# Attention and expert layer on one core: the mixed query tile transposed with 128 rows, the last output tile projected with 128 columns

## The chip, the cores and the metric

The kernel runs on one core of a Trainium2 chip. The metric is the device time of one execution in microseconds (us). The time before is 489.7 us, the median of three runs (489.33 to 493.12).

## What is computed

Attention with pooled queries, followed by a mixture of experts. Batch 2, 8 heads, 1152 positions, head size 64; everything is float32.

```python
q_pool = q.reshape(B, H, S // 2, 2, D).mean(axis=3)            # 576 queries a head
scores = np.matmul(q_pool, k.transpose(0, 1, 3, 2)) / np.sqrt(D)
attn = softmax(scores)                                        # over 1152 keys
x = heads side by side of np.matmul(attn, v)                  # (1152, 512)
expert = argmax(x @ w_gate); gate = its softmax probability
out[i] = gate[i] * (relu(x[i] @ w1[expert]) @ w2[expert])     # 8 experts, 512 -> 1024 -> 512
```

An expert takes no more than 288 tokens, in the order of the tokens; a token past that gives zeros.

## The kernel before, in words

The attention stage works on eight pairs of heads (2 batches, 4 pairs each). A pair's 576 pooled queries are four tiles of 128 and a rest of 64 (`MIX`, line 45) for each head. The two rests of 64 share one tile, the mixed query tile: its first 64 rows belong to the first head of the pair, its last 64 to the second. So a pair has nine query tiles, and each is worked through in three rounds of 384 keys, 27 rounds a pair.

In a round (`rounds`, lines 686 to 749) TensorE issues, in an order written out by hand: some matmuls of transposed probabilities with values (`pv_kt`, line 434); the score matmuls of the round six ahead (`s_third`, line 371), two terms for a plain tile and three for the mixed one; and three transposes of probabilities (`t_round`, line 409). VectorE takes the maximum of each score third (line 376), ScalarE the exponential (line 392, three rounds ahead); a score buffer is free for a new third when its exponential is done, and there are four. ScalarE and VectorE take turns at copying transposed probabilities out (lines 420 and 418).

Between the rounds stands the preparation of the next pair: the keys are transposed in three parts (`prep_k`, line 217), the pooled queries in two (`prep_q`). The first part of `prep_q` transposes two full query tiles (line 243). The second (`r == 1`) transposes two more full ones (line 243) and then the rest (line 249): 64 rows, both heads' columns side by side, through the 64 x 64 corner of the identity. ScalarE copies 256 or 320 columns out (line 257), and VectorE and GpSimd split them into high and low parts (lines 267 and 273). The pooled queries themselves are sums of neighbours, made by GpSimd into the tile `qp` (lines 204 and 207; for the first pair by VectorE, lines 200 and 324). `qp` has one buffer, requested anew for each pair (line 195).

What leaves attention goes through `x_out` (lines 447 to 486): the products `xt`, copied from PSUM by ScalarE (line 442), are transposed back and multiplied with the gate's weights in one matmul a tile (line 464) against `wgi`, an identity of 128 columns with the 16 gate columns beside it. A float32 matmul is two matmul instructions in the trace. Each pair calls `x_out` twice: for query tiles 0 and 1 (two full tiles) at the end of its own rounds, and for tiles 2, 3 and the rest (two full tiles and one with 64 weight columns) in round 17 of the next pair. The last pair is taken apart (`TAIL`, line 640): its rest is a call of its own (group 3), at the end of attention. `xt` has 320 columns and two buffers. The copies behind `x_out` (lines 473 and 479, VectorE) read 128 rows of full tiles and 64 rows of the rest.

Routing (lines 488 to 560) follows per batch, on VectorE with two small matmuls (lines 523 and 524), and scatters the tokens to their experts' slots by GpSimd (line 551). Then come the experts (lines 839 to 978), whose weights stream in through SyncE's queue (line 620) into 16 buffers. How many blocks of tokens an expert has is known on the chip alone, so blocks behind the first stand under a branch (line 950).

The order of instructions is by hand on TensorE throughout; in the main rounds also on ScalarE and VectorE; in the expert stage on GpSimd, SyncE, ScalarE and TensorE. Elsewhere a planner orders them by estimated costs.

Of the kernel before, what the change touches and what calls it, by code (L numbers as in the profile page):

```python
# [8 lines left out]
F32 = mybir.dt.float32  # L9
# [22 lines left out]
def f32(ap):  # L32
    return ap.bitcast(F32)
# [3 lines left out]
def attention_moe(ctx: ExitStack, tc, cap, q, k, v, wg, w1, w2, out):  # L37
    nc = tc.nc
    B, H, S, D = q.shape
    SQ = S // 2  # L40
    E, DM, F = w1.shape
    P = 128
    KT = S // P
    QT = SQ // P
    MIX = SQ - QT * P
    NT = QT + 1
    G0 = 2 * P
    GW = (G0, SQ - G0)
    W = P + 2 * E
# [12 lines left out]
    ident = const.tile([P, P], F32, name="ident")  # L62
# [22 lines left out]
    wgi = const.tile([P, HP, W], F32, name="wgi")  # L85
# [31 lines left out]
    ld_p = a_ctx.enter_context(tc.tile_pool(name="ld", bufs=1))  # L117
# [3 lines left out]
    sm_p = a_ctx.enter_context(tc.tile_pool(name="sm", bufs=4))  # L121
# [66 lines left out]

    ready = {}
    qps = {}  # L190
    pool_ins = [None]

    def prep_pool(p):
        kraw, qraw, vraw = raws[p]
        qp = ld_p.tile([P, NT, 2, D], F32, tag="qp", name="qp")
        qo = qp.rearrange("p t h d -> p h t d")
        qps[p] = qp
        if p == 0:
            for t in (0, 2):
                nc.vector.tensor_tensor(  # L200
                    out=qo[:, :, t:t + 2], in0=qraw[:, :, t:t + 2, 0:D], in1=qraw[:, :, t:t + 2, D:2 * D], op=ALU.add
                )
            return
        nc.gpsimd.tensor_tensor(
            out=qo[0:MIX, :, QT], in0=qraw[0:MIX, :, QT, 0:D], in1=qraw[0:MIX, :, QT, D:2 * D], op=ALU.add
        )
        pool_ins[0] = nc.gpsimd.tensor_tensor(
            out=qo[:, :, 0:QT], in0=qraw[:, :, 0:QT, 0:D], in1=qraw[:, :, 0:QT, D:2 * D], op=ALU.add
        ).ins
# [27 lines left out]
    def prep_q(p, r):  # L237
        qp = qps[p]
        qa, qb = q1[p % nbuf]
        ps = m_ps.tile([P, 512], F32, tag="t", name="qps")  # L240
        sc = 1.0 / 16.0
        for i in range(2):
            nc.tensor.transpose(
                ps[:, i * P:(i + 1) * P], qp[:, 2 * r + i].rearrange("p h d -> p (h d)"), ident
            )
        n = 2 * P
        spans = [[(0, n, 2 * r * P)] for _ in range(2)]
        if r == 1:
            nc.tensor.transpose(
                ps[:, n:n + MIX], qp[0:MIX, QT].rearrange("p h d -> p (h d)"), ident[0:MIX, 0:MIX]  # L250
            )
            spans = ([(0, n + MIX, n)], [(0, n, n), (n, n + MIX, QT * P + MIX)])
            n += MIX
        qt_s = ld_p.tile([P, CW], F32, tag="qts", name="qts", bufs=2)

        def post():
            nc.scalar.activation(qt_s[:, 0:n], ps[:, 0:n], AF.Copy, scale=sc)

            def split(j, tl):
                ready[p] = ready.get(p, 0) + 1  # L260
                if True:
                    rs = slice(j * D, (j + 1) * D)
                    for r0 in (slice(0, D), slice(D, P)):
                        for a, z, o in spans[j]:
                            c = slice(o, o + z - a)
                            if p:
                                nc.vector.tensor_copy(tl[r0, 0, c], qt_s[rs, a:z])  # L267
                            else:
                                nc.scalar.copy(tl[r0, 0, c], qt_s[rs, a:z])
                    for r0 in (slice(0, D), slice(D, P)):  # L270
                        for a, z, o in spans[j]:
                            c = slice(o, o + z - a)
                            nc.gpsimd.tensor_tensor(  # L273
                                out=tl[r0, 1, c], in0=qt_s[rs, a:z], in1=f32(tl[rs, 0, c]), op=ALU.subtract
                            )

            return slot_of_dve(lambda: split(0, qa), lambda: split(1, qb))

        return post
# [147 lines left out]
    def pv_kt(p, grp, kt):  # L427
        vraw = raws[p][2]
        if kt == 0:
            pvps[0] = (t_ps if grp == 3 else v_ps).tile([P, 512], F32, tag="t" if grp == 3 else "v", name="pv")  # L430
        ps = pvps[0]
        src, c0, n, _ = GRP[grp]
        for j in range(2):
            nc.tensor.matmul(  # L434
                ps[j * D:(j + 1) * D, 0:n], vraw[:, j, kt, :], pts[p, j, src][:, kt, c0:c0 + n],
                start=kt == 0, stop=kt == KT - 1,
            )
        if kt == KT - 1:
            xt = sm_p.tile([P, GW[1]], F32, tag="xt", name="xt", bufs=2)

            def post():
                nc.scalar.copy(xt[:, 0:n], ps[:, 0:n])  # L442

            xts[p, grp] = xt
            return post

    def x_out(p, grp):
        b, hp = divmod(p, HP)
        sm = sums[p]
        cuts = GRP[grp][3]  # L450
        if cuts[-1] == LAST[0]:
            nc.gpsimd.tensor_copy(sm[0:MIX, QT, 1, 0:3], sm[MIX:P, QT, 0, 0:3])
        t0, t1 = cuts[0][0], cuts[-1][1]
        z = sm_p.tile([P, 3, 2], F32, tag="z", name="z")
        zr = z[:, 0:t1 - t0]
        nc.vector.tensor_reduce(out=zr, in_=sm[:, t0:t1, :, 0:3], axis=AX.X, op=ALU.add)
        nc.vector.tensor_scalar_add(zr, zr, 1e-9)
        nc.vector.reciprocal(zr, zr)
        xt = xts.pop((p, grp))
        ps = m_ps.tile([P, 512], F32, tag="t", name="xps")  # L460
        for t in range(t0, t1):
            i = t - t0
            w = P if t < QT else MIX
            nc.tensor.matmul(
                ps[0:w, i * W:(i + 1) * W], xt[:, i * P:i * P + w], wgi[:, hp, :], start=True, stop=True
            )

        def post():
            for a0, a1, rows in cuts:
                nt = a1 - a0  # L470
                src = ps[0:rows, (a0 - t0) * W:(a1 - t0) * W].rearrange("p (t w) -> p t w", w=W)
                zz = z[0:rows, a0 - t0:a1 - t0, :].unsqueeze(3)
                nc.vector.tensor_tensor(
                    out=lp[0:rows, b, a0:a1, :, 2 * hp:2 * hp + 2].rearrange("p t e h -> p t h e"),
                    in0=src[:, :, P:W].rearrange("p t (h e) -> p t h e", h=2),
                    in1=zz.to_broadcast([rows, nt, 2, E]),
                    op=ALU.mult,
                )
                nc.vector.tensor_tensor(
                    out=x_tok[0:rows, b, a0:a1, hp * P:(hp + 1) * P].rearrange("p t (h d) -> p t h d", h=2),  # L480
                    in0=src[:, :, 0:P].rearrange("p t (h d) -> p t h d", h=2),
                    in1=zz.to_broadcast([rows, nt, 2, D]),
                    op=ALU.mult,
                )

        return slot_of_dve(post)
# [91 lines left out]
    for done in range(0, E * cap, nz * P):  # L578
        n = min(nz * P, E * cap - done)
# [46 lines left out]
    with ExitStack():  # L626
        load_pair(0)
        prep_pool(0)
        first = prep_first()
        load_pair(1)  # L630
# [55 lines left out]
        def rounds(n0, n1):  # L686
            nonlocal posts
            for n in range(n0, n1):
# [32 lines left out]
                if 0 <= p < NP:  # L721
                    if i == XO0 and p < NP - 1:
                        todo.append(lambda: x_out(p, 0))
                    if i == 26 and p % HP == HP - 1 and p < NP - 1:
                        todo.append(lambda b=p // HP: routing(b, 0, 2))
                    if p + 1 < NP:
                        pk, pq, p0 = (PK, PQ, 1) if p else (PK0, PQ0, PP0)
                        if i in pk:
                            todo.append(lambda: prep_k(p + 1, pk.index(i)))
                        if i in pq:  # L730
                            todo.append(lambda: prep_q(p + 1, pq.index(i)))
                        if i == p0:
                            prep_pool(p + 1)
                        if i == 25:
                            todo.append(lambda: prep_mix(p + 1))
                    if p == 0 and i == 6:
                        todo.append(lambda: prep_mix(0))
                    if i == 10 and p + 2 < NP:
                        load_pair(p + 2)
                    if p in (1, 2) and i % 3 == 0:  # L740
                        fill()
                    while fills and p == 2 and i == NS - 1:
                        fill()
                    if p == NP - 2 and i % 2 == 0 and i // 2 < NR0:
                        load_w(i // 2)
# [258 lines left out]
```

## Time and profile before

| what | value |
|---|---|
| median of three runs | 489.7 us (489.33 to 493.12) |
| the profiled execution | 491.99 us |
| its span, first to last instruction | 490.3 us |
| mean granted TensorE clock | 0.974 of full speed |
| TensorE matmuls busy | 449.8 us, 92% |
| VectorE, ScalarE, GpSimd busy | 245.9, 251.1, 170.9 us |

The profile is of one execution. PE is TensorE's matmuls, PEld its weight loads, which overlap with matmuls; DVE is VectorE, ACT ScalarE, POOL GpSimd, SP SyncE. L464 is line 464 of the kernel. Matmuls are pipelined and their ends are modelled, so a busy TensorE isn't one at its peak.

### The profile page before, as it was taken

To read this page: it belongs to the slowest core of one execution; us is meant where nothing else is said; L and a number is where in the kernel's file an instruction comes from. 1 tells how busy PE (TensorE), PEld (TensorE's weight loads), DVE (VectorE), ACT (ScalarE), POOL (GpSimd) and SP (SyncE) were. 2 spreads that over 40 slices of the span, in tenths; PEclk is the share of its full clock that TensorE was granted. 3 is DMA by queue.
4 is the path that set the end of the run, shared out by engine and by line. 5 is a ranking of instruction groups with operands and counts; after the bars stand their busy time and mean duration, and the time that the engine had idled before them with its cause. 6 is when DMAs were issued, how large, how long until landed. Compare 5 with 4: busy or idle time off the path is not lost. (4 is left out here: it accounts for less than half of the span.)

```text
span 490.3 us, 9116 instructions
## 1 busy us (share of the span) xinstructions
PE 449.8 (92%) x3183; PEld 315.5 (64%) x3183; DVE 245.9 (50%) x725; ACT 251.1 (51%) x731; POOL 170.9 (35%) x290
## 2 busy tenths in 40 slices
PE   4779999999999999999999998996999999999990
PEld 3667777777677677677776765464668456674670
DVE  5687777777777999887777565010100011001100
ACT  5777887787787677777777761020221112101100
POOL 4477444344344454454433001522031133112110
PEclk9799999999999999999999999798999999999996
DMA  7998984033043044052104625699983093000000
GB/s 216 276 284 282 385 285 108 5 98 100 5 98 102 1 119 124 3 150 55 30 20 139 260 70 204 215 341 355 363 285 145 5 364 123 13 12 24 12 11 21
DMA packets 55737, 69.96 MB, mean 143 GB/s; under 512 B 21873, under 2 KB 32117, under 8 KB 55680
## 3 DMA queue, kind: packets, MB, share of 16 engines
q1 hardware_dynamic: 50320, 53.56, 35.5%
q0 software_dynamic: 4816, 15.66, 8.5%
q8 instruction: 32, 0.52, 0.4%
q14 instruction: 25, 0.20, 0.1%
q10 hardware_dynamic: 544, 0.02, 0.1%
HBM read 52.48 MB, written 11.98 MB: 131 GB/s over the span
## 5 line engine op out<-in xcount | busy, mean ns | idle before, releaser
L376 DVE TENSOR_REDUCE negm<-s 128x1 f32<-128x384 f32 x216 | 119.6, 554 | 56.9 <-PE s L371 55.8
L371 PE MATMUL s<-k,q 128*128 128x384 f32 x432 | 132.8, 390 | 9.6 <-ACT p L392 9.0
L392 ACT ACTIVATE p<-s,negm 128x384 f32<-128x384 f32 x216 | 125.0, 587 | 14.6 <-DVE negm L380 9.2
L409 PE MATMUL tp<-ident,p 128*128 128x128 f32 x648 | 106.8, 274 | 0.5 <-DVE pt L418 0.4
L371 PEld LDWEIGHTS s<-k,q 128*128 128x128 f32 x432 | 66.8, 194 | 45.3 <-ACT p L392 25.2
L409 PEld LDWEIGHTS tp<-ident,p 128*128 128x128 f32 x648 | 83.9, 141 | 10.0 <-issue 1.4
L420 ACT COPY pt<-tp 128x384 f32<-128x384 f32 (+1 forms) x160 | 69.3, 445 | 38.5 <-PE tp L409 35.5
L434 PE MATMUL pv<-pt,vraw 128*64 128x256 f32 (+2 forms) x612 | 85.4, 403 | 0.8 <-ACT xt L442 0.8
L273 POOL TENSOR_TENSOR q<-qts,q 64x256 fp32r<-64x256 f32 (+1 forms) x76 | 52.0, 693 | 55.0 <-DVE q L267 47.8
L229 POOL TENSOR_TENSOR k<-kts,k 64x384 fp32r<-64x384 f32 x42 | 44.8, 1068 | 53.7 <-DVE k L228 51.9
L890 PE MATMUL hps<-wraw,xf 128*64 128x256 f32 (+1 forms) x448 | 49.7, 390 | 8.1 <-PEq L950 4.6
L828 POOL DMA_INDIRECT out_dram<-yo,id x17 | 17.1, 1006 | 112.9 <-issue 42.5
L434 PEld LDWEIGHTS pv<-pt,vraw 128*64 128x64 f32 x612 | 36.3, 136 | 27.2 <-issue 10.6
L930 PE MATMUL yps<-wraw,ht 128*64 128x256 f32 (+1 forms) x448 | 48.1, 382 | 1.2 <-DVE ht L907 1.2
L895 DVE TENSOR_SCALAR hs<-hps 128x256 f32<-128x256 f32 x12 | 5.1, 425 | 87.9 <-PE hps L890 87.9
L890 PEld LDWEIGHTS hps<-wraw,xf 128*64 128x64 f32 (+1 forms) x448 | 30.5, 136 | 26.5 <-issue 7.5
L392 ACT ACTIVATION_READ_ACCUMULATOR p<-s,negm 128x1 f32 x216 | 44.5, 206 | 0.0
L418 DVE COPY pt<-tp 128x384 f32<-128x384 f32 (+1 forms) x80 | 40.0, 508 | 6.1 <-PE tp L409 6.0
L822 ACT ACTIVATE yo<-yps,gt 128x256 f32<-128x256 f32 (+1 forms) x15 | 7.7, 516 | 61.5 <-PE yps L930 31.1
L930 PEld LDWEIGHTS yps<-wraw,ht 128*64 128x64 f32 (+1 forms) x448 | 28.4, 133 | 16.8 <-ACT ht L909 1.8
L849 PEld LDWEIGHTS hps<-xf,wraw 128*128 128x128 f32 x192 | 21.7, 192 | 1.2 <-issue 1.2
L849 PE MATMUL hps<-xf,wraw 128*128 128x128 f32 x192 | 22.2, 277 | 0.0
(117 smaller groups left out, 377.0 us busy)
## 6 DMA issues: line engine op xcount, KB each, us to landing
wraw<-in_moe_w_dram SPq DMA_DIRECT2D x32, 1024.0 KB, 7.9
vraw<-in_v_dram SPq DMA_DIRECT2D x8, 576.0 KB, 4.0
kc<-k SPq DMA_DIRECT2D x16, 288.0 KB, 4.0
xs<-zrow POOLq DMA_DIRECT2D x4, 1032.0 KB
qraw<-in_q_dram SPq DMA_DIRECT2D x16, 256.0 KB, 3.6
kraw<-in_k_dram SPq DMA_DIRECT2D x14, 288.0 KB, 4.6
xe<-xs POOLq DMA_DIRECT2D x14, 258.0 KB, 6.0
out_dram<-zrow POOLq DMA_DIRECT2D x2, 1024.0 KB
```

What stands on the lines that cost most here:

```text
L229: nc.gpsimd.tensor_tensor(out=tl[rl, c], in0=kt_s[rh, :], in1=f32(tl[rh, c]), op=ALU.subtract)
L273: nc.gpsimd.tensor_tensor(out=tl[r0, 1, c], in0=qt_s[rs, a:z], in1=f32(tl[rs, 0, c]), op=ALU.subtract)
L371: nc.tensor.matmul(ps[:, 0:CW], a, w, start=i == 0, stop=i == len(terms) - 1)
L376: nc.vector.tensor_reduce(out=negm3[g][:, j:j + 1], in_=ps[:, 0:CW], axis=AX.X, op=ALU.max, negate=True)
L392: nc.scalar.activation(pexp[g][:, j * CW:(j + 1) * CW], sthird.pop(n)[:, 0:CW], AF.Exp, bias=negm3[g][:, 3:4], scale=1.0, accum_out=sums[p ...
L409: nc.tensor.transpose(ps[:, i * P:(i + 1) * P], pexp[g][:, kt * P:(kt + 1) * P], ident)
L418: nc.vector.tensor_copy(dst, sr)
L420: nc.scalar.copy(dst, sr)
L434: nc.tensor.matmul(ps[j * D:(j + 1) * D, 0:n], vraw[:, j, kt, :], pts[p, j, src][:, kt, c0:c0 + n], start=kt == 0, stop=kt == KT - 1,)
L849: at = nc.tensor.matmul(ps[:, i * n:(i + 1) * n], raw[c][:, d, i * P:(i + 1) * P], xf[:, d, o:o + n], start=d == 0, stop=d == DC - 1,)
L890: at = nc.tensor.matmul(ps[g * n:(g + 1) * n, 0:256], xf[:, d, o:o + n], raw[c // 512][:, d, c % 512:c % 512 + 256], start=d == 0, stop=d ...
L930: nc.tensor.matmul(ps[k:k + n, 0:256], ht[:, j, g * n:(g + 1) * n], raw[2 + r // 512][:, r % 512 // P, c * 256:(c + 1) * 256], start=i == ...
```

## The change

The mixed tile's transpose takes all 128 rows of `qp`, whose rows 64 to 127 of the last tile are set to zero once, at the start; `qp` becomes one fixed tile. The projection of the rest takes 128 columns of `xt`; `xt` becomes two fixed tiles of 384 columns, set to zero once at the start and used in turn. The results in the additional columns and rows aren't read.

```diff
     ready = {}
     qps = {}
+    qp = ld_p.tile([P, NT, 2, D], F32, name="qp")
+    nc.gpsimd.memset(qp[MIX:P, QT], 0.0)
+    xt_s = [sm_p.tile([P, 3 * P], F32, name=f"xt{i}", bufs=1) for i in range(2)]
+    for t in xt_s:
+        nc.gpsimd.memset(t, 0.0)
     pool_ins = [None]
 
     def prep_pool(p):
         kraw, qraw, vraw = raws[p]
-        qp = ld_p.tile([P, NT, 2, D], F32, tag="qp", name="qp")
         qo = qp.rearrange("p t h d -> p h t d")
...
         if r == 1:
-            nc.tensor.transpose(
-                ps[:, n:n + MIX], qp[0:MIX, QT].rearrange("p h d -> p (h d)"), ident[0:MIX, 0:MIX]
-            )
+            nc.tensor.transpose(ps[:, n:n + P], qp[:, QT].rearrange("p h d -> p (h d)"), ident)
             spans = ([(0, n + MIX, n)], [(0, n, n), (n, n + MIX, QT * P + MIX)])
             n += MIX
...
         if kt == KT - 1:
-            xt = sm_p.tile([P, GW[1]], F32, tag="xt", name="xt", bufs=2)
+            xt = xt_s[0]
+            xt_s.reverse()
...
         for t in range(t0, t1):
             i = t - t0
-            w = P if t < QT else MIX
-            nc.tensor.matmul(
-                ps[0:w, i * W:(i + 1) * W], xt[:, i * P:i * P + w], wgi[:, hp, :], start=True, stop=True
-            )
+            nc.tensor.matmul(ps[:, i * W:(i + 1) * W], xt[:, i * P:(i + 1) * P], wgi[:, hp, :], start=True, stop=True)
```

## Rows read from the trace of the kernel before

**Rows 1.** The page, part 1: busy us, share of the span, instructions.

```profile
PE 449.8 (92%) x3183; PEld 315.5 (64%) x3183; DVE 245.9 (50%) x725; ACT 251.1 (51%) x731; POOL 170.9 (35%) x290
```

**Rows 2.** Busy table: us; PE, PEld, DVE, ACT, POOL busy; clock; DMA share; GB/s.

```profile
100.00:150.00 50.00, 49.59 (x340) 37.16 (x340) 37.09 (x105) 38.06 (x114) 22.52 (x29) 1.00 0.29 74
```

**Rows 3.** Waits: who waited for whom, us in total, times, longest.

```profile
DVE negm L376 <- PE s L371: 55.8, 74, 2.2
...
ACT pt L420 <- PE tp L409: 35.5, 63, 2.6
...
POOL qp L204 <- PE qps L249: 14.2, 5, 3.5
...
PE s L371 <- ACT p L392: 9.0, 17, 1.9
```

**Rows 4.** Groups by form, whole span: count, busy us, mean ns, idle before.

```profile
L464 PEld LDWEIGHTS xps<-wgi,xt 128*128 128x128 f32 x64 | 8.7, 190 | 0.5
...
L464 PE MATMUL xps<-wgi,xt 128*64 128x144 f32 x16 | 3.7, 312 | 0.0
...
L249 PE MATMUL qps<-ident,qp 64*128 64x64 f32 x8 | 2.3, 283 | 0.0
...
L464 PEld LDWEIGHTS xps<-wgi,xt 128*64 128x64 f32 x16 | 1.5, 134 | 1.2
```

**Rows 5.** Timeline of TensorE at a second query part: start us, duration, instructions merged.

```profile
77.72 0.38 PE L243 MATMUL qps<-ident,qp 128*128 128x128 f32 x2
78.03 0.27 PE L249 MATMUL qps<-ident,qp 64*128 64x64 f32 x1
...
78.69 0.34 PE L371 MATMUL s<-kc,qc 128*128 128x384 f32 x1
```

**Rows 6.** Timeline of TensorE at a first query part, which has full tiles only.

```profile
93.14 0.38 PE L243 MATMUL qps<-ident,qp 128*128 128x128 f32 x2
...
93.71 0.27 PE L409 MATMUL tp<-ident,p 128*128 128x128 f32 x1
```

**Rows 7.** Timeline of TensorE at a projection with the rest; last row: narrower window.

```profile
73.72 1.04 PE L464 MATMUL xps<-wgi,xt 128*128 128x144 f32 x6
...
75.15 0.34 PE L371 MATMUL s<-kc,qc 128*128 128x384 f32 x1
...
73.72 0.53 PE L464 MATMUL xps<-wgi,xt 128*128 128x144 f32 x3
```

**Rows 8.** Timeline of TensorE at a projection of two full tiles.

```profile
85.99 0.74 PE L464 MATMUL xps<-wgi,xt 128*128 128x144 f32 x4
...
86.92 0.38 PE L409 MATMUL tp<-ident,p 128*128 128x128 f32 x2
```

**Rows 9.** Timeline of TensorE behind the first mixed transpose, at the start.

```profile
17.40 0.98 PE L371 MATMUL s<-k,q 128*128 128x384 f32 x2 [0.51 <-ACT p L392]
```

**Rows 10.** Timeline of the tail of attention.

```profile
300.73 1.15 PE L464 MATMUL xps<-wgi,xt 128*128 128x144 f32 x6
...
301.63 0.41 DVE L479 TENSOR_TENSOR x_tok<-xps,z 128x256 f32<-128x256 f32 x1
...
303.82 0.25 PE L523 MATMUL rps<-oh,upper 128*128 128x16 f32 x1 [1.62 <-DVE r L503]
```

**Rows 11.** Timelines of VectorE and TensorE behind one pair's two edited places.

```profile
81.64 0.56 DVE L376 TENSOR_REDUCE negm<-s 128x1 f32<-128x384 f32 x1 [0.76 <-PE s L371]
...
84.14 0.62 PE L371 MATMUL s<-k,q 128*128 128x384 f32 x2 [0.27 <-ACT p L392]
```

**Rows 12.** Timeline of GpSimd at the start.

```profile
3.66 0.52 POOL L574 MEMSET zrow<- 128x516 f32 x1
...
10.94 2.92 POOL L309 TENSOR_TENSOR k<-kts,k 64x384 fp32r<-64x384 f32 x3 [6.60 <-ACT k L308]
```

**Rows 13.** Timeline of TensorE in the expert stage: a wait at a branch, a usual batch.

```profile
338.52 5.36 PE L890 MATMUL hps<-wraw,xf 128*64 128x256 f32 x32 [4.58 <-PEq L950]
...
348.34 3.62 PE L890 MATMUL hps<-wraw,xf 128*64 128x256 f32 x32
```

## The prediction

> **What bounds the kernel now.** I read the page first. The busy line has TensorE at 92% of the span and VectorE and ScalarE near 50% [rows 1]. An average over stages proves little, so next came the busy table by stretch: from 100 to 150 us, in the middle of the attention loop, the matmul row is busy 49.59 of 50 us at the full 2.4 GHz (granted clock 1.00), VectorE and ScalarE about 37 to 38 [rows 2]. Then the table of waits: VectorE's score maximum waits 55.8 us in all for the score matmuls, ScalarE's copies 35.5 us for the transposes, while TensorE's matmuls wait for ScalarE's exponentials 9.0 us in all, 17 times [rows 3]. So in attention the others follow TensorE, and what TensorE saves there should come off the end. Last came the groups by form and the timeline of TensorE around the two places that the diff touches.
>
> A reader needs one caution here. The matmul row is "busy" while a matmul is still draining, and ends overlap, so durations (283 and 312 ns [rows 4]) aren't the price of an instruction. I price by start-to-start distance.
>
> **Part 1, the mixed query tile (line 249, 8 times).** Eight 64-row transposes become 128-row ones; the instruction count stays. Beside the pooled query's last tile, two 128-row transposes (line 243) lead, one 64-row one follows, then the score matmuls. From the first of the lead to the third score matmul it takes 78.69 - 77.72 = 0.97 us [rows 5]. The other half of the same preparation has no 64-row transpose: from its first lead transpose to the operation behind the same two score matmuls it takes 93.71 - 93.14 = 0.57 us [rows 6]. One 128-row transpose behind another adds 0.38 us (two of them together) less 0.27 us (one alone, the last row there), about 0.11 us [rows 6]. After the change: 0.57 + 0.11 = 0.68 us. Saved: 0.29 us a time. What goes is the gap on both sides of the odd shape: the 64-row transpose starts 0.31 us behind the first lead transpose [rows 5], where two steps of 0.11 would put it at 0.22, and the first matmuls behind it start late as well.
>
> **Part 2, the last output tile (line 464, 8 times two matmuls).** Here two matmuls with 64 weight columns get 128; each tile's product is two matmuls in the trace, 16 narrow ones in all [rows 4]. Now: from the first of six matmuls to the third score matmul, 75.15 - 73.72 = 1.43 us [rows 7]. Three full ones take 0.53 us together [rows 7]; less the 0.29 us of one, and halved, that is a step of 0.12 us. After the change there are five such steps, 0.61 us, and then the way out. That I take from the sister call, which projects full tiles alone: its four end 85.99 + 0.74 = 86.73, so the last began at 86.44, and the operation behind two score matmuls starts at 86.92 [rows 8], 0.48 us later. (Its first matmul is not used, since it waited for its input.) Sum 0.61 + 0.48 = 1.09, saved 0.34 us.
>
> **The sum.** Of the eight calls of part 1, the first lies at the start, where the next score matmul waits 0.51 us for an exponential [rows 9] and nothing is won; seven lie in the loop: 7 x 0.29 = 2.0 us. Of the eight of part 2, seven lie in the loop: 7 x 0.34 = 2.4 us. The eighth lies in the tail: its six matmuls end at 300.73 + 1.15 = 301.88, but VectorE is busy with the tiles before until 301.63 + 0.41 = 302.04, and TensorE later waits 1.62 us for VectorE [rows 10]. So nothing there. Sum: 4.4 us. The bounds: a loss of 16 x (190 - 134) ns = 0.9 us, if no gap goes and the wider loads [rows 4] stand on the path; at most a gain of 16 x 0.34 = 5.4 us, if every call counts as the dearer kind. I take 4.4, since both distances after the change come from rows in which exactly these full shapes follow one another.
>
> Does it stay saved? Score matmuls wait now and then for an exponential to free their buffer, some 0.27 us as at 84.14. If that wait were set by ScalarE alone, TensorE would only arrive earlier and wait longer. But VectorE, one link up in that chain, itself idled 0.76 us for score matmuls at 81.64 [rows 11], behind both edits of that pair (73.7 and 78.0). The chain starts at TensorE and moves with it. So I take the gain as kept, and keep "half lost" as a rival.
>
> The weights of part 2 are wider, and here a rule speaks against the change. The full loads take 190 ns and the narrow ones 134 [rows 4], but full ones follow each other with their matmuls at 0.12 us [rows 7], so the loads lie beside matmuls and I add nothing for them. The Trainium skill, TensorE: Matmul & The Clock Gate, section LDWEIGHTS (loading the stationary operand), says that a load's time goes with its columns; the trace agrees with that in size, and were the difference exposed, the 14 loads in the loop at 0.056 us each, 0.8 us, would go from the sum, 486.1 us in place of the forecast.
>
> **What is added.** Three memsets on GpSimd at the start. No row has their shapes; the nearest is the 516-column memset, 0.52 us [rows 12], so between nothing and 1.6 us for the three. GpSimd then idles 6.60 us before its first real subtraction at 10.94 [rows 12], which hides all of it; without that cover the start would move by up to 1.6 us. Behind them on GpSimd's queue lie only small fills until then. The waits that they add (TensorE's and ScalarE's first use of the two output buffers) end tens of us before those uses. No DMA is issued, moved or passed. The reads of the copies behind both edits keep their 320 columns and 64 rows, so ScalarE and VectorE cost the same. The pooled query is now one fixed buffer, as it had one before: GpSimd's next pooled sum waited for the 64-row transpose already (14.2 us, 5 times [rows 3]) and goes on to wait for its successor.
>
> The profiled execution took 491.99 us, 490.3 of it span; so I expect a span of 485.9. The median of the runs shown is 489.7, 2.3 below that execution; the saving doesn't depend on which, and the forecast is 489.7 - 4.4 = **485.3 us**.
>
> **Rivals.**
> 1. *Half is lost to ScalarE and VectorE.* For it: those waits for the exponentials, and the routing work that crowds VectorE. Against it: VectorE's idling above. Time 489.7 - 2.2 = 487.5.
> 2. *Nothing changes*, because the odd shape's cost is not its shape but the wait behind it (a change that doesn't do what it says). For it: the rows can't separate shape from what follows. Against it: score matmuls follow full shapes in [rows 6] and [rows 8] without the gap. 489.7.
> 3. *The expert stage takes it back.* There, at 338.52, TensorE idled 4.58 us behind a branch, and the 32 matmuls after took 5.36 us where such a batch takes 3.62: 4.58 + 1.74 = 6.3 us [rows 13]. The attention stage's end moves relative to weight transfers already under way, and a second such wait may appear, at any of the experts' branches: 485.3 + 6.3 = 491.6, slower. It decides as soon as a new wait exceeds 4.4 us. Against it: the weight loads of that stage are issued behind the same work and move along.
> 4. *The same wait shrinks*, by the same argument: down to 479.0 if it goes wholly.
>
> **How the numbers follow.** Forecast 0.60 (own range 484.6 to 486.2), half lost 0.15, no change 0.06, taken back 0.09, shrunk 0.10. The range takes in rival 1 and most of the spread of rival 4, and leaves most of 3 and some of 2 outside: 483.3 to 489.2. About 1% (4.9 us, 484.8) is what a measurement can tell from no change. The forecast lies 0.9% below before, just inside it; of its 0.60 I give 0.24 to beyond 1%, and with rival 4 that makes 0.34 faster. Slower by over 1% (above 494.6) needs rival 3 without most of the gain: 0.05. The rest, 0.61, is within.
>
> **What would show it.** Right: at the mixed transpose 0.68 us from the first lead transpose to the third score matmul, at the projection 1.09 us; both groups of narrow forms gone from the groups by form; the distance of a pair of heads shorter by 0.63 us; expert stage starting some 4.4 us earlier. Wrong: these distances as before (rival 2); distances shorter but longer waits of score matmuls for exponentials (rival 1); attention shorter and the expert stage longer (rival 3).

## The result and the profile after

The changed kernel takes 483.75 us (480.95 to 485.19, four runs) against 490.1 us before (489.33 to 493.12, four runs): a ratio of 0.985, 95% interval 0.981 to 0.989. An unchanged copy timed later gave 0.983 (0.980 to 0.987). The forecast had 485.3, a gain of 0.9% and most likely within 1%; it came out as a gain of 1.5%, clearly beyond. The time lies inside the range but below the forecast's own 484.6 to 486.2, the likeliest class was the wrong one, and about a third of the gain has another origin than the prediction named.

TensorE's share on the page is as it was in kind, with 8.4 us less matmul time; GpSimd has three instructions more:

```profile
PE 441.4 (91%) x3183; PEld 312.0 (65%) x3183; DVE 244.7 (51%) x725; ACT 251.5 (52%) x731; POOL 171.9 (36%) x293
```

The busy table in the middle of the attention loop (columns as in [rows 2]) still has TensorE full. More rounds fit into the same 50 us, which is why VectorE and ScalarE rise by about 1 us each:

```profile
100.00:150.00 50.00, 49.59 (x349) 37.80 (x348) 38.27 (x109) 39.12 (x116) 23.39 (x29) 1.00 0.31 78
```

At the mixed transpose, TensorE's timeline of the changed kernel answers to [rows 5] (line 247 is the old 243, line 253 the old 249, line 373 the old 371):

```profile
76.90 0.38 PE L247 MATMUL qps<-ident,qp 128*128 128x128 f32 x2
77.12 0.27 PE L253 MATMUL qps<-ident,qp 128*128 128x128 f32 x1
...
77.58 0.34 PE L373 MATMUL s<-kc,qc 128*128 128x384 f32 x1
```

From the first lead transpose to the third score matmul: 77.58 - 76.90 = 0.68 us, where [rows 5] has 0.97. The third transpose now starts 0.22 us behind the first, two usual steps.

At the projection, the timeline that answers to [rows 7]:

```profile
73.24 0.90 PE L466 MATMUL xps<-wgi,xt 128*128 128x144 f32 x6
...
74.33 0.34 PE L373 MATMUL s<-kc,qc 128*128 128x384 f32 x1
```

74.33 - 73.24 = 1.09 us, where it was 1.43. The groups by form hold no narrow or short form any more; compare [rows 4]:

```profile
L466 PE MATMUL xps<-wgi,xt 128*128 128x144 f32 x80 | 13.2, 295 | 0.0
L466 PEld LDWEIGHTS xps<-wgi,xt 128*128 128x128 f32 x80 | 10.7, 190 | 0.5
...
L253 PE MATMUL qps<-ident,qp 128*128 128x128 f32 x8 | 2.3, 290 | 0.0
```

The waits that answer to [rows 3]:

```profile
DVE negm L378 <- PE s L373: 52.2, 70, 1.9
ACT pt L422 <- PE tp L411: 30.8, 60, 2.6
...
PE s L373 <- ACT p L394: 9.7, 18, 2.3
```

VectorE and ScalarE wait less for TensorE, TensorE 0.7 us more for exponentials. That is all that went to rival 1.

**Where the time went.** The two profiled spans differ by 7.2 us (490.3 and 483.1). The trace places them; times are in us from the span's start, the last column is what was gained since the mark above:

| mark | before | after | gained in the stretch |
|---|---|---|---|
| first projection (line 464, after the change 466) | 51.03 | 50.55 | 0.48 |
| last projection | 301.59 | 296.83 | 4.28 |
| first transpose of the experts (line 802) | 315.33 | 310.07 | 0.50 |
| start of the last matmul of the experts | 478.65 | 473.89 | -0.50 |
| start of the last scatter (line 828) | 480.79 | 476.04 | -0.01 |
| end of the span | 490.27 | 483.06 | 2.46 |

The loop gave what was forecast. The expert stage took half a microsecond back, which is less than two traces of one kernel differ by (163.3 and 165.2 us for the kernel before). The surprise is the last row: behind the last scatter, with all arithmetic done, the kernel before needed 9.48 us to its end and the changed one 7.02. Three views show where. The last row of the timeline is the scatter itself (start, duration); the view of line 950 has the branch code with the sequencers' instructions, that of line 1000 the end of the program (durations in ns; the times behind are first and last start in us). First the kernel before:

```profile
480.79 0.98 POOL L828 DMA_INDIRECT out_dram<-yo,id  x1 [13.64 <-ACTq L950]
```

```profile
L950 POOLq EVENT_SEMAPHORE  x1: 17/17/17, 483.2 to 483.2; - x1
L950 POOLq INC_SWDGE_SEM  x1: 1279/1279/1279, 483.3 to 483.3; - x1
```

```profile
L1000 POOLq DRAIN  x3: 46/109/4644, 484.8 to 490.0; - x3
```

The same three of the changed kernel:

```profile
476.04 0.98 POOL L828 DMA_INDIRECT out_dram<-yo,id  x1 [13.64 <-POOLq L950]
```

```profile
L950 POOLq EVENT_SEMAPHORE  x1: 17/17/17, 476.0 to 476.0; - x1
L950 POOLq INC_SWDGE_SEM  x1: 1264/1264/1264, 476.1 to 476.1; - x1
```

```profile
L1000 POOLq DRAIN  x3: 46/112/4644, 477.6 to 482.8; - x3
```

GpSimd's program ends with a semaphore instruction beside the scatter, another of 1.3 us, and a drain of 4.64 us. In the changed kernel the semaphore instruction runs beside the scatter (476.0); before, it came 2.4 us after the scatter's start (483.2), and the drain, which decides the end, slid with it (484.8 is 4.0 behind the scatter, 477.6 is 1.5). None of these rows shows what it waited for; a view of the packets does, further below. The scatter's row says the same from the other side: its last releaser is GpSimd's own sequencer after the change, ScalarE's before. In the table of waits and in the chain this can't be seen at all, since instructions that only wait aren't work.

### The profile page after: what moved, and what is told of

The parts are those of the page before. It is cut to its first block, busy times and chain, and to the rows that moved or that the text cites. A ratio compares the mean times of both kernels' runs of the same rounds, so it can differ in the third digit from the quotient of the medians.

```text
span 483.1 us, 9114 instructions
## 1 busy us (share of the span) xinstructions
PE 441.4 (91%) x3183; PEld 312.0 (65%) x3183; DVE 244.7 (51%) x725; ACT 251.5 (52%) x731; POOL 171.9 (36%) x293
## 5 line engine op out<-in xcount | busy, mean ns | idle before, releaser
L373 PE MATMUL s<-k,q 128*128 128x384 f32 x432 | 131.1, 387 | 10.1 <-ACT p L394 9.7
```

Source lines behind the costliest of these rows:

```text
L373: nc.tensor.matmul(ps[:, 0:CW], a, w, start=i == 0, stop=i == len(terms) - 1)
```

## The experiments

The expectations name four theories. A: the odd shapes' gaps in the loop are all that the change gives. B: the extra 2.5 us at the end belong to GpSimd's program, whose last instructions come sooner because others were put ahead of them. C: they come with the planner's other order of transfers and pooled sums (below). D: they fall by chance from execution to execution.

**Each part alone.** First the mixed transpose only:

```diff
+    qp = ld_p.tile([P, NT, 2, D], F32, name="qp")
+    nc.gpsimd.memset(qp[MIX:P, QT], 0.0)
...
+            nc.tensor.transpose(ps[:, n:n + P], qp[:, QT].rearrange("p h d -> p (h d)"), ident)
```

> Only the mixed query tile's transpose takes 128 rows (one memset added). Theory A (what is saved is the odd shapes' gaps in the attention loop, the rest of the measured gain is elsewhere): seven times 0.29 us, attention ends 2.0 us earlier, ratio 0.996. Theory B (about 2 us of the gain come at the very end of the program, where GpSimd's last instructions come sooner because three instructions were added to its program): 2.0 us in the loop, and part or none of the end's 2.4 us, since one instruction is added in place of three. Theory C (the extra gain comes with the other order of transfers and pooled sums, which this kernel has too): 2.0 us in the loop and 2 us more, ratio 0.992.

Measured: 0.990 (0.986 to 0.993). In its trace the first and last projection start at 50.08 and 298.54, a stretch of 248.5 us; 250.3 in the unchanged copy below, 250.6 in the kernel before. So 1.8 to 2.1 us, where six transposes lie in the stretch (6 x 0.29 = 1.74). The end behind the last scatter is 7.02 us. The ratio is worth 5.1 us of the 491.83 that the kernel before took beside it (29 runs): more than the loop, and about right with the end. Theory A's 0.996 lies outside the interval.

Then the projection only:

```diff
+    xt_s = [sm_p.tile([P, 3 * P], F32, name=f"xt{i}", bufs=1) for i in range(2)]
+    for t in xt_s:
+        nc.gpsimd.memset(t, 0.0)
...
+            nc.tensor.matmul(ps[:, i * W:(i + 1) * W], xt[:, i * P:(i + 1) * P], wgi[:, hp, :], start=True, stop=True)
```

> Only the last output tile's projection takes 128 columns (two memsets added; the order of transfers stays). Theory A: seven times 0.34 us, attention ends 2.4 us earlier, and up to 0.3 in the tail, ratio 0.995. Theory B: the same in attention, and part or none of the 2.4 us at the end, two instructions being added. Theory C: 2.4 us alone, 0.995.

Measured: 0.991 (0.987 to 0.995), 4.3 us. First to last projection 50.73 to 298.72, 248.0 us: 2.3 less than the copy, as 7 x 0.34 = 2.4. The end again 7.02. This kernel has the old order of transfers, and yet the early end, so theory C isn't needed for it; by the time alone theory C's 0.995 lies at the edge of the interval.

**The memsets alone**, on GpSimd, with nothing that reads them and no matmul changed:

```diff
+    idle = sm_p.tile([P, 3 * P], F32, name="idle", bufs=1)
+    nc.gpsimd.memset(idle[MIX:P, 0:P], 0.0)
+    for _ in range(2):
+        nc.gpsimd.memset(idle, 0.0)
```

> The kernel before with three memsets of the same sizes on GpSimd that nothing reads; no matmul is changed. Theory A and C: no change, ratio 1.000, the expert stage begins where it did (315.3 us). Theory B: attention as before, and the end of the program some 2.4 us shorter behind the last scatter (9.5 us before, 7.0 after the change), ratio 0.995.

Measured: 0.995 (0.992 to 0.999), 2.3 us faster by adding three instructions that do nothing. First to last projection 49.85 to 300.07, 250.2 us, as in the copy. The end is 7.02 us; the scatter starts at 476.40, and in the view of line 950 (954 here) the semaphore instruction stands beside it:

```profile
L954 POOLq EVENT_SEMAPHORE  x1: 17/17/17, 476.4 to 476.4; - x1
```

**The changed kernel with its memsets on VectorE:**

```diff
-    nc.gpsimd.memset(qp[MIX:P, QT], 0.0)
+    nc.vector.memset(qp[MIX:P, QT], 0.0)
...
-        nc.gpsimd.memset(t, 0.0)
+        nc.vector.memset(t, 0.0)
```

> The changed kernel with its three memsets on VectorE, so that GpSimd's program has as many instructions as before. Theory A and C: as the changed kernel, ratio 0.985 to 0.990, end behind the last scatter as it falls. Theory B: the attention gain of 4.4 to 4.8 us alone, the end 9.5 us behind the last scatter as before, ratio 0.990.

Measured: 0.988 (0.983 to 0.994), end 7.02 us. Theory B as I had put it failed here. Counting GpSimd's records in the trace, with those that only wait, showed why it need not have: this kernel executes 506 and not 503 as the kernel before, because the fixed query tile brings three more waits (part 1 alone has 507, with one memset). So the next runs varied the count itself.

**The unchanged copy, one more, one fewer, and the changed kernel again.**

> The kernel before once more, unchanged, as a control. If the 9.5 us between the last scatter's start and the end of the program belong to where GpSimd's instructions lie in its program (theory B, in the form: any instruction added ahead moves them), they are there again: 9.5 us. If they fall by chance from execution to execution (theory D), 7.0 us is as likely. Ratio 1.000 within 0.004 either way.

> The kernel before with a single memset on GpSimd at the start that nothing reads. Theory B: the end behind the last scatter is 7.0 us, ratio 0.995. Theory D: 7.0 or 9.5 us by chance, ratio 1.000. Attention and expert stage as before in both.

> The kernel before with one of its own memsets (the 128 x 128 of the triangle) moved from GpSimd to VectorE, so that GpSimd has one instruction fewer ahead. Theory B: the late instruction is still late, since it and its neighbour change sides by one place only: 9.5 us, ratio 1.000. If just any other program ends sooner: 7.0 us, 0.995. Theory D: by chance.

> The changed kernel once more, unchanged. Theory B: end behind the last scatter 7.0 us, attention ends 4.3 to 4.8 us before that of the unchanged copy, ratio 0.985 to 0.990. Theory D: end 7.0 or 9.5 by chance, and the ratio nearer 0.990.

The edits of the middle two:

```diff
+    nc.gpsimd.memset(idle[MIX:P], 0.0)
```

```diff
-    nc.gpsimd.memset(f32(upper), 1.0)
+    nc.vector.memset(f32(upper), 1.0)
```

The copy took 0.999 (0.996 to 1.002), with 9.77 us behind the last scatter; so the late instruction is no chance of one execution. With one memset more 0.999 (0.996 to 1.002) and 9.64 us: late still, against what I expected. With one memset moved away 0.994 (0.991 to 0.996) and 7.02 us: early, against what I expected. The changed kernel's copy 0.983 and 7.02 us. The row of the semaphore instruction in the same view (line 952), one memset more, where the scatter starts at 479.36:

```profile
L952 POOLq EVENT_SEMAPHORE  x1: 17/17/17, 482.0 to 482.0; - x1
```

One memset fewer, scatter at 481.18:

```profile
L950 POOLq EVENT_SEMAPHORE  x1: 17/17/17, 481.2 to 481.2; - x1
```

Both misses have the same sense: it isn't "any edit", and it isn't one place exactly. The kernel with one memset fewer executes 500 on GpSimd (its waits changed too), the one with one more 504. If the count decides, 503 and 504 are late, and 500, 505, 506, 507 and 509 early. That can be tested from the other side, by taking the *changed* kernel back to the bad counts.

**The changed kernel, taken back.** Its three memsets on VectorE and then two, and three, of the older ones as well:

```diff
-    nc.gpsimd.memset(f32(upper), 1.0)
+    nc.vector.memset(f32(upper), 1.0)
...
-    nc.gpsimd.memset(zrow, 0.0)
+    nc.vector.memset(zrow, 0.0)
```

> The changed kernel with its three memsets and two older ones (triangle, zero row) on VectorE: GpSimd executes 504 instructions, as many as in the kernel before with one memset added, which ended late. Theory B (where GpSimd's last instructions lie decides): end behind the last scatter 9.5 us again, attention gain kept, ratio 0.990. Rival (any program but the old one ends soon, or the new order of pooled sums and transfers did it): 7.0 us, ratio 0.985.

> As the last one, with one more memset (a quarter of the query padding) moved to VectorE: 503 instructions on GpSimd, as many as the kernel before executes. Theory B: end 9.5 us behind the last scatter, ratio 0.990. Rival: 7.0 us, ratio 0.985.

The first took 0.993 (0.990 to 0.996), the second 0.989 (0.986 to 0.992; by the medians of all its runs, 487.4 against 490.7, it is 0.993), and the end is 9.77 and 9.64 us: late again, with the loop's gain kept (last projection at 296.56 and 296.55, from a first one at 50.28 and 50.27). Their counts turned out as 503 and 502, each one below what I had worked out. The view of line 950 of the first, whose scatter starts at 475.72:

```profile
L950 POOLq EVENT_SEMAPHORE  x1: 17/17/17, 478.4 to 478.4; - x1
```

All kernels together, by GpSimd's executed count:

| GpSimd executes | kernels | end behind last scatter |
|---|---|---|
| 500 | one memset fewer | 7.02 |
| 502 | taken back, three | 9.64 |
| 503 | before, its copy, taken back, two | 9.48, 9.77, 9.77 |
| 504 | one memset more | 9.64 |
| 505 | part 2 alone | 7.02 |
| 506 | memsets alone; memsets on VectorE | 7.02, 7.02 |
| 507 | part 1 alone | 7.02 |
| 509 | the changed kernel, its copy, the two below | 7.02 each |

So in these kernels the end is early or late by where GpSimd's last instructions lie in its program. The order of transfers and of pooled sums doesn't decide it, nor does the gain in the loop: each occurs with either end. Chance from execution to execution (theory D) would hardly have sorted fourteen traces so.

The traces also show what the late instruction comes with. The DMA view counts the packets that carry instructions, by queue (packets, MB, share). From 470 us to the end, the kernel before has

```profile
q8 instruction: 1, 0.02, 0.4%
q14 instruction: 2, 0.02, 0.2%
```

and the changed one the first of these rows alone:

```profile
q8 instruction: 1, 0.02, 0.7%
```

The same view sorts all fourteen traces: two packets on queue 14 in each of the five with a late end, none in the nine with an early one. In the late ones the first of the two starts 0.8 to 1.1 us behind the scatter's start (before: 481.56). The semaphore instruction starts 2.4 to 2.7 us behind the scatter, but always 1.28 to 1.36 us behind that packet's end; it keeps its distance to the packet and not to the scatter. The second packet follows the semaphore instruction by 0.62 to 0.64 us. By this timing, what the late instruction waits for is its code. The packets don't name the engine that they serve, and why these places in the program need a late transfer and their neighbours don't, no run shows.

**Is it the array shape?** To vary the rows alone, two kernels do the mixed transpose as a plain matmul of two instructions, with 64 or 128 rows of weights, by the same 64 streamed columns:

```diff
+            nc.tensor.matmul(
+                ps[:, n:n + MIX], qp[0:MIX, QT].rearrange("p h d -> p (h d)"), ident[0:MIX, 0:MIX], start=True, stop=True
+            )
```

(`0:MIX` twice becomes `:` in the second.)

> The changed kernel with the mixed transpose done as a plain matmul (two instructions) of 64 rows by 64 streamed columns. If the gap belongs to the number of weight rows differing from that of its neighbours: about 0.31 us from the first lead transpose to the odd matmul, and from the first lead transpose to the third score matmul 0.97 us plus one more instruction, 1.0 to 1.2 us. If it belonged to the few columns or to the transpose mode beside other modes: the same distance as the next kernel.

> The same plain matmul with all 128 rows by the same 64 streamed columns; nothing else differs from the last kernel. If the rows make the gap: it follows the lead transposes at the usual step (0.22 us behind the first) and the third score matmul stands 0.7 to 0.85 us behind it. If the few columns make it: as the last kernel, 1.0 to 1.2 us.

TensorE's timeline with 64 rows, then with 128:

```profile
77.98 0.38 PE L247 MATMUL qps<-ident,qp 128*128 128x128 f32 x2
78.29 0.43 PE L253 MATMUL qps<-ident,qp 64*128 64x64 f32 x2
...
79.11 0.34 PE L375 MATMUL s<-kc,qc 128*128 128x384 f32 x1
```

```profile
77.12 0.38 PE L247 MATMUL qps<-ident,qp 128*128 128x128 f32 x2
77.34 0.33 PE L253 MATMUL qps<-ident,qp 128*128 128x64 f32 x2
...
77.92 0.34 PE L375 MATMUL s<-kc,qc 128*128 128x384 f32 x1
```

1.13 us against 0.80, and 0.31 against 0.22 us to the odd instruction. The streamed columns are the same; only the rows differ. All six sites in the loop have the same distances, within 0.01 us. Over the stretch from first to last projection it is 249.0 against 247.0 us, six times 0.34. The single times (487.5 and 483.7, one run each) point the same way. So a lone matmul with 64 weight rows among neighbours with 128 costs about 0.3 us more, on both sides of it. For 64 weight columns there is the comparison before and after alone: 0.34 us for the two matmuls of a product.

## Why the prediction was right and wrong, by its own steps

*Parts 1 and 2* held to the hundredth: 0.68 and 1.09 us forecast, 0.68 and 1.09 measured. They did, because both distances were taken from places in the same trace where only full shapes follow one another. The rule of the Trainium skill, TensorEngine Tiling (Array Packing), section Key Properties, is that changing the tiling mode drains TensorE. The last two runs agree as far as the time goes, at about 0.1 us in front of the odd instruction and 0.2 behind it, though no row shows a drain as such. The rule that the prediction had weighed against the change (the Trainium skill, TensorE: Matmul & The Clock Gate, section LDWEIGHTS) is that a load's time goes with its columns. The loads did grow, from 134 to 190 ns, but that cost nothing here: the way over the projection took the 1.09 us that were forecast without it.

*The sum* for the loop held: between first and last projection six transposes and seven projections, 6 x 0.29 + 7 x 0.34 = 4.1 us; measured 4.3 in the first pair of traces and 4.0 between the two copies (250.28 and 246.32). *Does it stay saved?* It did; TensorE's wait for exponentials grew by 0.7 us in all. Rival 1 fell with that, and rival 2 with the distances.

*What is added* is the step that failed. It priced three memsets on GpSimd by what they do: at nothing, since GpSimd idles behind them. They take 0.97 us and are hidden, just so:

```profile
3.77 0.20 POOL L192 MEMSET qp<- 64x128 f32 x1
4.02 0.77 POOL L195 MEMSET xt<- 128x384 f32 x2
```

What wasn't priced is that they, and three more waits for the fixed query tile, move every later instruction of GpSimd's program, and that the kernel before happened to lie at one of three bad places out of those tried. With that term, -2.5 us, the working gives 490.3 - 4.4 - 2.5 = 483.4 us for the span; measured 483.1. The end behind the last scatter, 9.5 us, was in the trace before, with the late semaphore instruction and the packets of code, and the prediction took it as a constant. Nothing there says that three memsets would shorten it: for the idea of the change this part of the gain is luck. The prediction also said "no DMA is issued, moved or passed"; that too was wrong in the letter, since the planner let the next pair's query load pass a copy of keys on SyncE's queue in four places, and exchanged two sums on GpSimd. Part 2 alone, without either, shows that nothing hangs on it.

*Rivals 3 and 4*, a wait at an expert's branch that grows or goes, both show in this pair of traces, and nearly cancel. TensorE in the expert stage of the changed kernel:

```profile
331.57 5.17 PE L890 MATMUL hps<-wraw,xf 128*64 128x256 f32 x32 [2.82 <-PEq L950]
...
353.47 0.87 PE L890 MATMUL hps<-wraw,xf 128*64 128x256 f32 x6 [1.34 <-ACT hs L897]
...
407.00 1.30 PE L890 MATMUL hps<-wraw,xf 128*64 128x256 f32 x10 [1.50 <-PEq L950]
```

The wait of 4.58 us ([rows 13]) shrank to 2.82, and two of 1.3 and 1.5 us came in where there were shorter ones or none. Both rivals had put that down to attention's end moving against the weight transfers. But the memsets alone, whose loop is as long as before, have the same at two of these places (line 894 there):

```profile
334.61 3.67 PE L894 MATMUL hps<-wraw,xf 128*64 128x256 f32 x32 [2.27 <-PEq L954]
...
407.37 3.67 PE L894 MATMUL hps<-wraw,xf 128*64 128x256 f32 x32 [1.89 <-PEq L954]
```

So a shorter loop isn't needed for it. From the experts' first transpose to the start of their last matmul the traces of all kernels range from 160.5 (memsets alone) to 165.6 us (part 2 alone), unchanged copies among them (163.3 and 165.2 for the kernel before). That spread is as large as the whole gain in the loop; with one trace of most kernels it can't be split into chance and program, and its cause stays open.

## What to carry to other kernels

A lone matmul with fewer weight rows or columns than its neighbours cost more here than a full one: price it by start-to-start distance on both sides, against a place in the same trace where only full shapes follow each other, and fill it up with zeros where these cost nothing. Before believing a gain of half a per cent, run the change's harmless parts alone: adding instructions that nothing reads made this kernel 0.5% faster. And look at what stands behind the last piece of work, up to the end of the span: no view of waits lists it, but the DMA view of the last microseconds shows packets of instructions that come late.

## What the runs showed of the hardware that was not expected

The end of the program behind the last scatter took 7.02 us in nine kernels' traces and 9.48 to 9.77 us in five, and the executed number of instructions on GpSimd separates them: 502 to 504 late, 500, 505, 506, 507 and 509 early. The late ones, and only they, have two packets of instructions on queue 14 behind the last scatter, and GpSimd's late instruction starts 1.28 to 1.36 us behind the end of the first. The long drain on GpSimd alone took 4.64 us in either case, so some 7 us of every profiled execution here lie behind the last scatter's start.
